# Sparse attention and Fourier mixing: batch 1's block sums and first mask on VectorE instead of GpSimd, its scaled sums on ScalarE instead of VectorE

## The chip, the cores and the metric

The kernel runs on one core of a Trainium2 chip. A core has a matmul engine (TensorE; PE in the profile, with its weight loads as PEld), VectorE (DVE), ScalarE (ACT), GpSimd (POOL) and SyncE (SP), which here issues nearly all DMAs. The metric is the device time of one execution in microseconds (us). The kernel before takes 800.13 us, the median of 3 runs (798.32 to 802.27).

## The reference

There are 4 batches of 8 heads, 768 tokens and 64 dimensions per head, in float32. The attention is local with a window of 16, plus one summary per block of 32 tokens: the key of a block is the maximum of its 32 keys, and its value is the mean of its 32 values. Its output, 768 tokens by 512 features, goes through a Fourier mixing, a normalisation and a two-layer network.

```
k_sum = k.reshape(B, H, nb, block, D).max(axis=3)
v_sum = v.reshape(B, H, nb, block, D).mean(axis=3)
scores_l = scale * np.matmul(q, k.transpose(0, 1, 3, 2))        # kept where |i - j| < 16
scores_s = scale * np.einsum('bhsd,bhnd->bhsn', q, k_sum) + np.log(block)
a = softmax over both;  x = a @ [v, v_sum], heads joined to (B, S, 512)
mixed = np.real(fft over tokens and features of x);  u = x + mixed
un = (u - mean) / sqrt(var + 1e-6)
out = u + relu(un @ w_ch1) @ w_ch2
```

The change touches how `v_sum` and the first masked local scores of batch 1 are computed.

## The kernel before, in words

Heads are handled in pairs (g = 0 to 3). Batch 0's attention (`first_attention`, L838) runs alone at the start, in blocks of 64 tokens; the other batches use blocks of 32 (`scores`, `sum_scores`, `scale_sums`, `values`, `gen_attention`). Batch 0's attention ends with the folding of its output for the Fourier transform (`fold_sequence`, `fold_halves`, `fold_ends`). Then the Fourier stage of batch 0 (`gen_fourier`, transforms `y` and `mx`, statistics, `norm`, transposes `unt` into `u`) runs interleaved with the conversion of the weights from 64-bit words (`convert`, L1069 to L1076) and with the attention of batch 1. After that, each batch's two-layer network runs interleaved with the attention of the next one.

`block_sums(b, gg)` (L610) serves the value sums for four heads, that is, for the pairs 2gg and 2gg+1. For b of 1 and more it fetches the values as 96 rows (4 heads by 24 blocks) in four pieces of 512 numbers (8 tokens each), `raw[0]` to `raw[3]`, and adds them on GpSimd: 0 and 1, 2 and 3, both results, and then the remaining 512 numbers by halving (256, 128, 64), to `vb`, 64 numbers for each block. `scale_sums` selects a pair's rows by a matmul (`sel`), and writes them to `vs` twice, multiplied by two columns of 0 and 1 (`half_of`): for batch 1 by one broadcast product on VectorE, for later batches by two activations with a scale on ScalarE. `values` uses `vs`.

`scores` computes the exponentials of the local scores on ScalarE and multiplies them by a mask (`near`). This product is on VectorE, except for pair 0 of batch 1, where it is on GpSimd (`gtt`, L569), queued behind the block sums (`marks["vbs", 1]`).

What sets the order of the work: the program is written in one order, and a planner fills each engine's queue from it, oldest ready operation first; a block under `high_priority` (the Fourier stage, 600) counts as older. A younger operation can go ahead of an older one that the planner takes as not ready yet. `manual_schedule` around `first_attention` keeps the order of its own TensorE and VectorE operations among themselves, but doesn't keep others from going between them. `issue_after(m)` queues operations behind a mark m on the same engine. DMAs through `fetch` (L551) keep their written order on SP's queue while `in_order` is set, as it is up to the first network stage. In that order, block sums (1, 0) are loaded behind the values of pair (1, 0), the tables `near` and `mirror`, two pieces of weights, and keys and queries of pair (1, 1); sums (1, 1) are loaded after the Fourier stage of batch 0 is written.

Records of `tt` have line L567 and those of `gtt` L570, whatever calls them; `fetch` has L553. The tiles tell them apart: `vb` and `vbs` are the block sums, `p<-p,near` the mask, `vs<-vs,half` the scaled product, `big<-x,norm` the normalised tile, `words` and `w` the weights.

Of the kernel before, what the change touches and what calls it, by code (L numbers as in the profile page):

```python
# [12 lines left out]
AF = mybir.ActivationFunctionType  # L13
ALU = mybir.AluOpType
AX = mybir.AxisListType

P = 128
# [473 lines left out]
def _main_program(ctx, tc, q, k, v, moe_w_ch1, moe_w_ch2, out):  # L491
# [59 lines left out]
    def fetch(out, in_):  # L551

        ins = nc.sync.dma_start(out=out, in_=in_)  # L553
        if in_order[0]:
            tc.keep_in_program_order(ins)
        return ins.ins
# [12 lines left out]
    def gtt(out, in0, in1, op):  # L569
        return nc.gpsimd.tensor_tensor(out=out, in0=in0, in1=in1, op=op).ins  # L570
# [39 lines left out]
    def block_sums(b, gg):  # L610

        heads, rows = slice(4 * gg, 4 * gg + 4), 4 * nb
        f = BLOCK // 4
        n = f * D
        vb = spool.tile([rows, D], FP, tag="vbs", bufs=2, name=f"vbs_{b}_{gg}")
        for g in (2 * gg, 2 * gg + 1):
            sums[b, g] = vb, sel[:, g % 2]
        src = v[b, heads].rearrange("h (n f) d -> (h n) (f d)", f=BLOCK)
        if b == 0:

            raw = words[0:rows, 4 * n * gg:4 * n * (gg + 1)]
            fetch(out=raw, in_=src)
            to_add[gg] = raw, vb
            return
        if done_weights:
            raw = room(f"vb_{b}_{gg}")
            raw = [raw[0:rows, n * i:n * (i + 1)] for i in range(4)]
        else:

            raw = [bpool.tile([P, NC, P], FP, tag="s", bufs=5, name=f"vb_{b}_{gg}_{i}").rearrange("p n t -> p (n t)")  # L630
                   [0:rows] for i in range(4)]
        for i in range(4):
            fetch(out=raw[i], in_=src[:, n * i:n * (i + 1)])

        gtt(raw[0], raw[0], raw[1], ADD)
        gtt(raw[2], raw[2], raw[3], ADD)
        gtt(raw[0], raw[0], raw[2], ADD)
        while f > 2:
            f //= 2
            gtt(raw[0][:, 0:f * D], raw[0][:, 0:f * D], raw[0][:, f * D:2 * f * D], ADD)  # L640
        marks["vbs", b] = gtt(vb, raw[0][:, 0:D], raw[0][:, D:2 * D], ADD)

# [124 lines left out]
    def scores(b, g):  # L769
        kt, qt = kt_bufs[g % 2], nat[b, g]  # L770
        ps = [abank([P, NB2, BLOCK], f"sc_{b}_{g}_{h}") for h in range(2)]
        for i in range(NB2):
            for h in range(2):
                o = BLOCK * (NB2 * h + i)
                for e in range(2):
                    rows, r = slice(D * e, D * (e + 1)), 64 * (e ^ h)
                    nc.tensor.matmul(ps[h][r:r + 64, i, :], kt[rows, o:o + 64], qt[rows, o:o + BLOCK],  # L777
                                     start=True, stop=True)
        p = apool.tile([P, 2, NQ, QB], FP, tag="p", name=f"p_{b}_{g}")
        pm = p[:, 1].rearrange("p n c -> p (n c)")[:, 0:S2]  # L780
        p = p[:, 0].rearrange("p (h i) (j c) -> p h (i j) c", h=2, c=BLOCK)
        for h in range(2):
            nc.scalar.activation(out=p[:, h], in_=ps[h], func=AF.Exp, scale=SC)
            with tc.issue_after(marks["vbs", 1]) if (b, g) == (1, 0) else ExitStack():
                (gtt if (b, g) == (1, 0) else tt)(p[:, h], p[:, h], near[:, h], ALU.mult)
        return p, pm

    def sum_scores(b, g, p):
# [8 lines left out]
    def scale_sums(b, g):  # L797
        ps = abank([P, D], f"vs_{b}_{g}")
        vb, pick = sums[b, g]
        nc.tensor.matmul(ps, pick, vb, start=True, stop=True)  # L800
        if b > 1:
            for r in range(2):
                nc.scalar.activation(out=vs[:, r, 0:D], in_=ps, func=AF.Identity, scale=half_of[:, r:r + 1])
        else:
            tt(vs[:, :, 0:D], ps[:, None, :].to_broadcast([P, 2, D]),
               half_of[:, :, None].to_broadcast([P, 2, D]), ALU.mult)

    def values(b, g, p, pm, x):
        vw = vw_bufs[g % 2]
# [28 lines left out]
    def first_attention():  # L838

        x = x_of[0] = bpool.tile([P, NST, DM], FP, tag="x", bufs=2, name="x_0")  # L840
        fold = bpool.tile([P, 7, 2, S2], FP, tag="u", name="fold_0").rearrange("p a k n -> p (a k n)")
        wt["fold"] = split_fold(0, fold)
        p = {0: wide_scores(0, 0, lambda: add_blocks(0))}
        prepare(0, 1)
        sum_values(0, 0)
        load(0, 3)
        for g in range(NP - 1):
            p[g + 1] = wide_scores(0, g + 1, (lambda: add_blocks(1)) if g == 1 else None)
            wide_values(0, g, p[g], x)
            load_values(*following(0, g, 2))  # L850
            for par in range(2):
                fold_sequence(par, g)
            if g < NP - 2:
                prepare(0, g + 2)
                sum_values(0, g + 1)
            if g == NP - 3:
                load(1, 0)
                get_tables(0, lambda: load_raw(1))
                load_raw(2)
                sum_values(0, g + 2)  # L860
        fold_halves(0, 0)
        wide_values(0, NP - 1, p[NP - 1], x)
        for par in range(2):
            fold_sequence(par, NP - 1)
            if par:
                fold_halves(par, 0)
            fold_halves(par, 1)
            for _ in fold_ends(0, par, wt["fold"][:, par], wt["fold"][:, 2 - 2 * par]):
                pass
# [96 lines left out]
    def gen_attention(b):  # L966
        x = bpool.tile([P, NST, DM], FP, tag="x", bufs=2, name=f"x_{b}")
        x_of[b] = x
        held = None
        if b == 2:  # L970
            load(2, 1)
            load(2, 2)
        if b > 1:
            yield
            yield
            with tc.issue_after(marks["load"]):
                block_sums(b, 0)
            for _ in range(2):
                yield
        for g in range(NP + 1):  # L980
            n1, n3 = (following(b, g, n) for n in (1, 3))
            if held:
                if b > 1:
                    scale_sums(b, g - 1)
                values(b, g - 1, *held, x)
                if n1 and b > 1:
                    load_values(*n1)
            if g == NP and b > 1:
                turn_tiles(b, x)
                for _ in range(17):  # L990
                    yield
                rooms[b] = room(f"fold_{b}")
                steps = fold_batch(b, split_fold(b, rooms[b]))
                while True:
                    with tc.issue_after(marks["dense"]):
                        done = next(steps, steps) is steps
                    if done:
                        break
                    yield
            elif held:  # L1000
                for _ in range(5 if b > 1 else 1):
                    yield
            if g < NP:
                held = scores(b, g)
                if (b, g) == (1, 1):
                    key_maxima(g)
                sum_scores(b, g, held[1])
            if g and n1 and b == 1:
                load_values(*n1)
            if g == 1 and b > 1:  # L1010
                block_sums(b, 1)
            if g == NP and b > 1:
                return
            yield
            if g == NP:
                return
            for _ in range(2 if g == 0 and b > 1 else 0):
                yield
            if n1:
                prepare(*n1, *((1,) if b > 1 else ()))  # L1020
            if b == 1:
                scale_sums(b, g)
            if b > 1:
                yield
                yield
                if n1:
                    prepare(*n1, 0)
            if n3 and not (b == 1 and n3 > (2, 0)):
                load(*n3)
            yield  # L1030
            if b > 1:
                yield
# [153 lines left out]
    def gen_fourier(b):  # L1186
# [45 lines left out]
        for half in range(2):  # L1232
# [46 lines left out]
            ins = nc.vector.tensor_tensor(out=z, in0=minus, in1=y, op=ALU.mult)  # L1279
            if b == 0:  # L1280
                marks["mx", 0] = ins.ins
            norms.append((y, z))
        issued.add(("mx", b))
        for j in range(3):
# [200 lines left out]
    weights = gen_weights()  # L1485
    with tc.manual_schedule(engines={mybir.EngineType.PE, mybir.EngineType.DVE}):
        first_attention()
    fetch(out=near, in_=dr["near"].ap().rearrange("p (h i) c -> p h i c", h=2))
    fetch(out=mirror, in_=dr["mirror"].ap())
    load_raw(4)  # L1490
    load(1, 1)
    nc.vector.memset(vs, 0.0)
    nc.vector.tensor_scalar(out=vs[:, :, D], in0=half_of, scalar1=float(BLOCK), scalar2=None, op0=ALU.mult)

    block_sums(1, 0)

    def second_attention():
        prepare(1, 0)
# [76 lines left out]
```

## Time and profile before

| | us |
|---|---|
| median of 3 runs | 800.13 (798.32 to 802.27) |
| the profiled execution | 801.87 |
| its span in the profile | 800.0 |
| TensorE busy in the span | 775.7 |
| VectorE busy | 499.2 |
| ScalarE busy | 229.0 |
| GpSimd busy | 60.9 |

The page gives busy time for each engine; TensorE's matmuls are pipelined, so its busy time isn't time at its peak. The rows of a timeline are: start (us from the span's start), duration, engine, line, operation, output tile <- input tiles with their shapes, and how often; in brackets stands how long the engine was idle before, and what ended that. A list of waits gives the engine, the tile and the line that waited, what it waited for, and us in total, times, and the longest. "Granted clock" is the share of TensorE's full clock. Windows of the span show the stages:

| stretch, us | TensorE busy | VectorE busy | ScalarE busy | GpSimd busy | granted clock |
|---|---|---|---|---|---|
| 48 to 60 (first transform) | 12.00 | 9.53 | 5.72 | 0 | 0.77 |
| 69 to 75 (statistics) | 5.96 | 5.97 | 1.77 | 4.13 | 1.00 |
| 75 to 80 (norm) | 0.21 | 5.00 | 0.86 | 3.08 | 0.74 |
| 80 to 94 (transposes, attention of pair 0) | 12.12 | 11.32 | 11.45 | 0 | 0.73 |
| 94 to 116 (network, first half) | 19.97 | 21.14 | 13.06 | 0 | 1.00 |
| 116 to 123 | 7.00 | 6.42 | 3.33 | 6.25 | 1.00 |
| 147 to 190 (first output stage) | 42.86 | 36.77 | 15.18 | 0 | 1.00 |

GpSimd's work from 69 to 78 us is block sums (1, 0) and the first mask of batch 1; from 116 to 123 us it is block sums (1, 1).

### The profile page before, as it was taken

To read this page: it belongs to the slowest core of one execution; us is meant where nothing else is said; L and a number is where in the kernel's file an instruction comes from. 1 tells how busy PE (TensorE), PEld (TensorE's weight loads), DVE (VectorE), ACT (ScalarE), POOL (GpSimd) and SP (SyncE) were. 2 spreads that over 40 slices of the span, in tenths; PEclk is the share of its full clock that TensorE was granted. 3 is DMA by queue.
4 is the path that set the end of the run, shared out by engine and by line. 5 is a ranking of instruction groups with operands and counts; after the bars stand their busy time and mean duration, and the time that the engine had idled before them with its cause. 6 is when DMAs were issued, how large, how long until landed. Compare 5 with 4: busy or idle time off the path is not lost.

```text
span 800.0 us, 14475 instructions
## 1 busy us (share of the span) xinstructions
PE 775.7 (97%) x5914; PEld 566.6 (71%) x5914; DVE 499.2 (62%) x1113; ACT 229.0 (29%) x515; POOL 60.9 (8%) x99
## 2 busy tenths in 40 slices
PE   8987899999999999999999999999999999999997
PEld 6776655445579866788569866688669875786686
DVE  5789898797988737663577635563576722532352
ACT  3542756445635112200226112210126102001200
POOL 0003011000000021200120020300030000000000
PEclk9989899999999999999999999999999999999999
DMA  9799596697756269985343169620613154106001
GB/s 227 170 270 206 158 275 174 233 252 263 214 164 173 68 171 208 251 137 138 134 174 138 54 198 194 176 82 1 229 57 139 46 189 144 70 0 231 0 28 55
DMA packets 133355, 121.84 MB, mean 152 GB/s; under 512 B 94464, under 2 KB 114912, under 8 KB 133088
## 3 DMA queue, kind: packets, MB, share of 16 engines
q1 hardware_dynamic: 132016, 118.53, 53.1%
q0 software_dynamic: 576, 2.10, 0.7%
q8 instruction: 48, 0.79, 0.4%
q10 hardware_dynamic: 688, 0.20, 0.1%
q14 instruction: 27, 0.22, 0.1%
HBM read 97.22 MB, written 23.59 MB: 151 GB/s over the span
## 4 chain that ended last, share of the span: by engine, by line
PE 85%; DVE 10%; ACT 3%; issue 1%; DMA 1%; ACTq 0%; DVEq 0%
PE hx L1325 19%; PE ox L1394 18%; PE hz L1325 9%; PE oz L1394 9%; PE oy L1394 5%; PE o L1371 4%; PE hy L1325 4%; PE y L1220 4%; PE mx L1179 2%; PE sc L777 2%; DVE w L567 2%; PE av L816 1%; PE unt L1299 1%; PE av L821 1%; DVE x L567 1%; DVE p L567 1%
## 5 line engine op out<-in xcount | busy, mean ns | idle before, releaser
L1325 PE MATMUL hx<-u,w 128*128 128x384 f32 x512 | 184.8, 490 | 4.9 <-DVE h L567 3.2
L1325 PEld LDWEIGHTS hx<-u,w 128*128 128x128 f32 x512 | 95.2, 190 | 73.7 <-DVE h L567 5.2
L1325 PE MATMUL hz<-u,w 128*128 128x384 f32 x256 | 93.5, 486 | 0.0
L1394 PE MATMUL oz<-w,s 128*128 128x256 f32 x336 | 81.5, 380 | 0.0
L1394 PE MATMUL ox<-w,s 128*128 128x256 f32 x336 | 80.3, 380 | 0.0
L1394 PE MATMUL ox<-w,h 128*128 128x256 f32 x336 | 79.9, 381 | 0.0
L567 DVE TENSOR_TENSOR x<-ox,x 128x256 f32<-128x256 f32 x84 | 35.4, 423 | 67.5 <-PE ox L1394 67.3
L1325 PEld LDWEIGHTS hz<-u,w 128*128 128x128 f32 x256 | 48.5, 190 | 34.3 <-ACT h L1344 0.9
L1394 PEld LDWEIGHTS ox<-w,h 128*128 128x128 f32 x336 | 63.0, 190 | 11.1 <-issue 1.2
L1394 PEld LDWEIGHTS ox<-w,s 128*128 128x128 f32 x336 | 63.0, 190 | 9.5 <-DVE x L567 0.8
L1394 PEld LDWEIGHTS oz<-w,s 128*128 128x128 f32 x336 | 63.4, 190 | 8.6
L1336 ACT COPY h<-hx 128x384 f32<-128x384 f32 x32 | 15.2, 476 | 184.6 <-PE hx L1325 184.6
L567 DVE TENSOR_TENSOR h<-hy,h 128x384 f32<-128x384 f32 x32 | 17.8, 556 | 47.3 <-PE hy L1325 47.2
L1325 PE MATMUL hy<-u,w 128*128 128x384 f32 x128 | 46.5, 486 | 0.0
L567 DVE TENSOR_TENSOR h<-hx,h 128x384 f32<-128x384 f32 x32 | 17.8, 556 | 43.3 <-PE hx L1325 43.2
L1371 PE MATMUL o<-w,h 128*128 128x512 f32 x96 | 42.2, 595 | 0.1
L1355 ACT ACTIVATE h<-hx 128x384 f32<-128x384 f32 x32 | 15.7, 491 | 88.4 <-PE hx L1325 88.4
L1394 PE MATMUL oy<-w,h 128*128 128x256 f32 x168 | 40.1, 380 | 0.0
L570 POOL TENSOR_TENSOR vb<-vb 96x512 f32<-96x512 f32 (+2 forms) x24 | 23.9, 997 | 179.7 <-DMA vb<-in_v_dram 178.3
L1325 PEld LDWEIGHTS hy<-u,w 128*128 128x128 f32 x128 | 24.3, 190 | 17.0
L567 DVE TENSOR_TENSOR x<-oz,x 128x256 f32<-128x256 f32 x42 | 17.8, 423 | 29.0 <-PE oz L1394 28.7
L1394 PEld LDWEIGHTS oy<-w,h 128*128 128x128 f32 x168 | 31.8, 190 | 4.4
(165 smaller groups left out, 1101.0 us busy)
## 6 DMA issues: line engine op xcount, KB each, us to landing
w<-dw SPq DMA_DIRECT2D x44, 896.0 KB, 5.6
words<-in_moe_w_ch_dram SPq DMA_DIRECT2D x32, 512.0 KB, 5.1
dw<-w SPq DMA_DIRECT2D x12, 896.0 KB, 6.9
vw<-in_v_dram SPq DMA_DIRECT2D x47, 192.0 KB, 5.7
out_dram<-x SPq DMA_DIRECT2D x23, 256.0 KB, 2.0
vb<-in_v_dram SPq DMA_DIRECT2D x24, 192.0 KB, 7.8
kn<-in_k_dram SPq DMA_DIRECT2D x9, 384.0 KB, 5.4
qn<-in_q_dram SPq DMA_DIRECT2D x9, 384.0 KB, 6.7
```

The source lines that it names most:

```text
L567: return nc.vector.tensor_tensor(out=out, in0=in0, in1=in1, op=op).ins
L570: return nc.gpsimd.tensor_tensor(out=out, in0=in0, in1=in1, op=op).ins
L777: nc.tensor.matmul(ps[h][r:r + 64, i, :], kt[rows, o:o + 64], qt[rows, o:o + BLOCK], start=True, stop=True)
L816: nc.tensor.matmul(av[r][32 * j:32 * (j + 1), t, :], p[rows, h, i - NB2 * h, :], vw[rows, i, :], start=(t == 0), stop=False, skip_group_ch ...
L821: ins = nc.tensor.matmul(av[r][:, t:t + HT + 1:HT, :], pm[rows, P * t:P * (t + 1)], vs[rows], start=False, stop=(t == HT - 1), skip_group_ ...
L1179: nc.tensor.matmul(out, y[:, g], table, start=False, stop=True, skip_group_check=True)
L1220: nc.tensor.matmul(y, fgs[b][par][:, st, P * g:P * (g + 1)], fs[par][:, g % 2, st, :], start=(st == 0), stop=(st == n - 1))
L1325: ins = nc.tensor.matmul(ps, w[:, a, kk, :], u[:, r, kk, :], start=start and kk == 0, stop=stop and kk == 1, skip_group_check=True)
L1336: nc.scalar.copy(out=c11, in_=X)
L1355: nc.scalar.activation(out=c21, in_=X, func=AF.Relu)
L1371: nc.tensor.matmul(ps, h[:, n, hf, P * t:P * (t + 1)], wt[2, b, j][:, 2 * hf:2 * hf + 2, :], start=(n, hf) == (0, 0), stop=(n, hf) == (NC ...
L1394: nc.tensor.matmul(ps, left[a][:, n, :], wt[2, b, j][:, r, :], start=start and n == 0, stop=stop and n == NC - 1, skip_group_check=True)
```

## The change

For batch 1 the block sums are added on VectorE: three additions of 96x512, and one reduction over the remaining 8 rows of 64 in place of the halving. For (1, 0) the loading and the adding are parted: the four loads are written in `first_attention` ahead of the loads of pair (1, 0)'s values, and the additions behind the end of `first_attention`, with no mark. For (1, 1) both stay where they were. The first mask of batch 1 moves to VectorE, behind the end of the norm of the first half (a new mark, `norm`), and is written after pair 0's scores and before the preparation of pair 1. The scaled sums of batch 1 are two activations on ScalarE, as in later batches. Later batches keep GpSimd for the block sums.

```diff
--- before.py
+++ after.py
@@ -631,14 +631,24 @@
                    [0:rows] for i in range(4)]
         for i in range(4):
             fetch(out=raw[i], in_=src[:, n * i:n * (i + 1)])
-
-        gtt(raw[0], raw[0], raw[1], ADD)
-        gtt(raw[2], raw[2], raw[3], ADD)
-        gtt(raw[0], raw[0], raw[2], ADD)
+        to_add[b, gg] = raw, vb
+        if (b, gg) != (1, 0):
+            add_later_blocks(b, gg)
+
+    def add_later_blocks(b, gg):
+        f = BLOCK // 4
+        raw, vb = to_add[b, gg]
+        add = gtt if b > 1 else tt
+        add(raw[0], raw[0], raw[1], ADD)
+        add(raw[2], raw[2], raw[3], ADD)
+        add(raw[0], raw[0], raw[2], ADD)
+        if b == 1:
+            nc.vector.tensor_reduce(out=vb, in_=raw[0].rearrange("p (f d) -> p d f", d=D), op=ADD, axis=AX.X)
+            return
         while f > 2:
             f //= 2
             gtt(raw[0][:, 0:f * D], raw[0][:, 0:f * D], raw[0][:, f * D:2 * f * D], ADD)
-        marks["vbs", b] = gtt(vb, raw[0][:, 0:D], raw[0][:, D:2 * D], ADD)
+        gtt(vb, raw[0][:, 0:D], raw[0][:, D:2 * D], ADD)
 
 
 
@@ -781,8 +791,8 @@
         p = p[:, 0].rearrange("p (h i) (j c) -> p h (i j) c", h=2, c=BLOCK)
         for h in range(2):
             nc.scalar.activation(out=p[:, h], in_=ps[h], func=AF.Exp, scale=SC)
-            with tc.issue_after(marks["vbs", 1]) if (b, g) == (1, 0) else ExitStack():
-                (gtt if (b, g) == (1, 0) else tt)(p[:, h], p[:, h], near[:, h], ALU.mult)
+            if (b, g) != (1, 0):
+                tt(p[:, h], p[:, h], near[:, h], ALU.mult)
         return p, pm
 
     def sum_scores(b, g, p):
@@ -798,12 +808,8 @@
         ps = abank([P, D], f"vs_{b}_{g}")
         vb, pick = sums[b, g]
         nc.tensor.matmul(ps, pick, vb, start=True, stop=True)
-        if b > 1:
-            for r in range(2):
-                nc.scalar.activation(out=vs[:, r, 0:D], in_=ps, func=AF.Identity, scale=half_of[:, r:r + 1])
-        else:
-            tt(vs[:, :, 0:D], ps[:, None, :].to_broadcast([P, 2, D]),
-               half_of[:, :, None].to_broadcast([P, 2, D]), ALU.mult)
+        for r in range(2):
+            nc.scalar.activation(out=vs[:, r, 0:D], in_=ps, func=AF.Identity, scale=half_of[:, r:r + 1])
 
     def values(b, g, p, pm, x):
         vw = vw_bufs[g % 2]
@@ -847,6 +853,8 @@
         for g in range(NP - 1):
             p[g + 1] = wide_scores(0, g + 1, (lambda: add_blocks(1)) if g == 1 else None)
             wide_values(0, g, p[g], x)
+            if g == NP - 2:
+                block_sums(1, 0)
             load_values(*following(0, g, 2))
             for par in range(2):
                 fold_sequence(par, g)
@@ -1016,6 +1024,10 @@
                 return
             for _ in range(2 if g == 0 and b > 1 else 0):
                 yield
+            if (b, g) == (1, 0):
+                for h in range(2):
+                    with tc.issue_after(marks["norm"]):
+                        tt(held[0][:, h], held[0][:, h], near[:, h], ALU.mult)
             if n1:
                 prepare(*n1, *((1,) if b > 1 else ()))
             if b == 1:
@@ -1279,6 +1291,7 @@
             ins = nc.vector.tensor_tensor(out=z, in0=minus, in1=y, op=ALU.mult)
             if b == 0:
                 marks["mx", 0] = ins.ins
+                marks["norm"] = marks.get("norm", ins.ins)
             norms.append((y, z))
         issued.add(("mx", b))
         for j in range(3):
@@ -1485,14 +1498,13 @@
     weights = gen_weights()
     with tc.manual_schedule(engines={mybir.EngineType.PE, mybir.EngineType.DVE}):
         first_attention()
+    add_later_blocks(1, 0)
     fetch(out=near, in_=dr["near"].ap().rearrange("p (h i) c -> p h i c", h=2))
     fetch(out=mirror, in_=dr["mirror"].ap())
     load_raw(4)
     load(1, 1)
     nc.vector.memset(vs, 0.0)
     nc.vector.tensor_scalar(out=vs[:, :, D], in0=half_of, scalar1=float(BLOCK), scalar2=None, op0=ALU.mult)
-
-    block_sums(1, 0)
 
     def second_attention():
         prepare(1, 0)
```

## The prediction

> **What bounds the kernel now.** I read the page first, for which engine is full, then the waits of TensorE, for where it is not.
>
> ```profile
> span 800.0 us, 14475 instructions
> PE 775.7 (97%) x5914; PEld 566.6 (71%) x5914; DVE 499.2 (62%) x1113; ACT 229.0 (29%) x515; POOL 60.9 (8%) x99
> ```
>
> TensorE stands still for 24.3 us of the span, so a change off TensorE can win only there, or where its clock is low. The waits of TensorE between 36 and 240 us have one long entry:
>
> ```profile
> PE unt L1299 <- DVE big L1294: 4.8, 1, 4.8
> PE hx L1325 <- DVE h L567: 2.5, 2, 1.4
> ...
> PE hx L1325 <- ACT h L1336: 1.7, 2, 1.1
> ```
>
> The first is batch 0's normalisation: TensorE ends its earlier work at 74.96 us (keys and queries of pair 1, which begin at 74.14 for 0.82) and turns the first normalised tile at 79.79. Third view, the timeline of VectorE and of GpSimd there (start, duration, engine, line):
>
> ```profile
> 69.58 0.91 DVE L1267 TENSOR_SCALAR stat<-both 128x3 f32<-128x3 f32 x1
> 70.40 0.15 DVE L1268 TENSOR_SCALAR stat<-both 128x3 f32<-128x3 f32 x1
> ...
> 72.14 1.14 DVE L567 TENSOR_TENSOR norm<-norm,stat 128x3 f32<-128x3 f32 x1
> ...
> 73.80 0.83 DVE L1278 SCALAR_TENSOR_TENSOR norm<-norm 128x3 f32<-128x3 f32 x1
> ...
> 76.18 2.08 DVE L1278 SCALAR_TENSOR_TENSOR norm<-norm 128x3 f32<-128x3 f32 x1
> ```
> ```profile
> 69.19 1.27 POOL L570 TENSOR_TENSOR vb<-vb,vb 96x512 f32<-96x512 f32 x1 [26.71 <-DMA vb<-in_v_dram]
> 71.98 2.63 POOL L570 TENSOR_TENSOR vb<-vb,vb 96x512 f32<-96x512 f32 x2 [1.52 <-DMA vb<-in_v_dram]
> ...
> 76.30 1.94 POOL L570 TENSOR_TENSOR p<-p,near 128x384 f32<-128x384 f32 x2
> ```
>
> Operations on three elements take 0.14 to 0.17 us when GpSimd is idle (L1268: 0.15), but four of them last until the GpSimd instruction beside them ends: 70.49 against 70.46, 78.26 against 78.24. The norm, and with it TensorE, stands behind the very work that this change takes off GpSimd. The chain that ended last runs through all four.
>
> **The stalls go.** (0.91-0.15) + (1.14-0.14) + (0.83-0.15) + (2.08-0.15) = 4.37 us. What is late next: the last of the matmuls that these sums read ends at 71.21 us (it starts at 70.18 and takes 1.03), and VectorE, relieved of the first two stalls, reaches the operation that reads it at 73.20-1.76 = 71.44, so it still doesn't wait; and TensorE is busy to 74.96 while the first tile would be ready at 79.79-4.37 = 75.42. So the whole 4.37 counts: -4.4.
>
> **Block sums of pairs 0 and 1 on VectorE.** Three additions of 96x512 and one reduction of 512 elements. The rows, first by group and shape (times, total us, mean ns of one, idle before), then by tile for the mask and for the product on ScalarE (minimum, median, maximum ns):
>
> ```profile
> L686 DVE TENSOR_REDUCE km<-kt 128x24 f32<-128x768 f32 x16 | 15.1, 944 | 0.3 <-ACT kt L713 0.3
> ...
> L567 DVE TENSOR_TENSOR words<-words 96x512 f32<-96x512 f32 x2 | 1.4, 686 | 0.1
> ```
> ```profile
> L567 DVE TENSOR_TENSOR p<-p,near x22: 548/551/1618, 96.7 to 526.4; 128x384 f32<-128x384 f32 x22
> ```
> ```profile
> L803 ACT ACTIVATE vs<-vs,half x16: 308/316/320, 302.8 to 528.1; 128x64 f32<-128x64 f32 x16
> ```
>
> A reduction of 512 with stride is not in the trace: from below 0.944 x 512/768 = 0.63, from above 0.944; I take 0.69, as an addition of 512 costs. So 4 x 0.69 = 2.7 us. They take the place of halving additions whose rows are 0.42, 0.29 and 0.22 (0.93 together).
> The Trainium skill, "VectorE: DVE Perf Modes", section "Rules for kernel authors", calls tensor_reduce the slowest VectorE operation and advises restructuring. By it the halving would stay, at 3 x 0.69 + 0.93 = 3.0 us instead of 2.7. The rows speak for the change: over 768 elements a reduction takes 0.944 us and an addition (L567, u) 0.950.
> Where do the first 2.7 us lie? Between the end of batch 0's folding (53.35) and the first sum of the norm (65.20) VectorE idles 2.20+0.38+0.71+0.55 = 3.84 us, by the waits in its timeline (ACT's conversions, then TensorE). That hides 2.7 us of work, but not a wait for the data as well. Data: the loads move ahead of the values' loads. The weights' load before them, issued at 39.90, lands 13.0 us later, at 52.9; 0.79 MB more at the 214 to 335 GB/s seen from 54 to 60 us lands at 55.3 to 56.6, if served in order. Additions that stand right behind the folding then wait 2 to 3.2 us: 2.7+3.2-3.84 = 2.1 at most, 0 at least; I take +0.5. Behind them the values' loads (used at 82.86), the mask (used at 76), the keys of pair 1 (used at 73.43) start some 3 us later: they landed by 59, 58.2 and 67.5, so this is hidden; without that cover each would cost its own lateness.
>
> **Sums (1,1), at 116 us.** GpSimd's work there stretches six VectorE operations by 0.24+1.08+1.07+0.53+0.25+0.12 = 3.3 us (against their rows of 0.42, 0.69, 0.68); 2.7 come instead: -0.6 on VectorE. TensorE waits 1.08 us for VectorE at 128.93. Between 0 and -1.1: I take -0.3.
>
> **Masks.** Two of 0.55 us, queued behind the first half's norm. Between 0 (in VectorE's 0.51 us wait at 80.93, and before the matmuls that need them at 82.86) and 1.1 (ahead of the first tile): +0.2.
>
> **Product on ScalarE.** Two of 0.316 for one of 0.285 on VectorE, four times. In the stretch 79.1 to 89.0 ScalarE never rests except 0.34+0.21 us waiting for TensorE's transposes, and the norm's further tiles and bank releases queue behind it: 0.63-0.55 = +0.1. The next, beside the copies of keys and queries at 92.8 to 97.0 after which TensorE waits 0.58 for ScalarE, 0 to 0.6; the last two 0 to 1.3, hidden under dense TensorE from 147 to 190 for one; together +0.3.
>
> **Clock.** The granted clock falls to 0.50 from about 77.5 us, 2.5 us into the wait, and is back at 1 by 88. Twelve transposes take 2.84 us at 79.79 and 1.66 at 87.37. With the wait near 0.4 us the clock should hold; ScalarE bounds that stretch, so of 1.2 I take -0.3 (from 0 to -3.5, half of the 7.08 us that TensorE worked from 80 to 88).
>
> Batches 2 and 3 keep their instructions; I cost them at nothing, since TensorE covers them (99% from 229 us on).
>
> **Sum.** -4.4 +0.5 -0.3 +0.2 +0.1 +0.3 -0.3 = -3.9 us. The profiled execution took 801.87 us (span 800.0, 1.87 around it): 798.0. It lies 1.74 above the median of the runs shown, 800.13, so against that: 796.2.
>
> **Rivals.** *Slower: the additions stand too early in VectorE's queue.* They bear no ordering tie to the folding, only the rule that the planner may fill an engine when an older operation is not ready. The trace shows both halves: VectorE's norm chain has later tiles' statistics threaded into it (L1254 between L1268 and L1271), and at the start VectorE waits 6.7 us, to 8.89, for a tiny load (L1493) with the first key maxima behind it. If the additions are planned for 44 to 50 us, VectorE stands until 55.3 to 56.6, and batch 0's folding, the first transform (TensorE from 48.09) and all else behind it: 5 to 12 us plus 2.7 of work, less the wait of 4.4 won: +3 to +10, about 805. It decides as soon as one addition stands ahead of the folding's last operation (52.88). Against it: the folding leaves VectorE 0.16 us of idle from 42 to 48 and none from 48 to 53, so hardly a place to fill.
> *Given back at 107 to 116.* The same for sums (1,1): their loads are issued from 107.26 and GpSimd starts only at 116.16 on the data. Additions planned at 111 to 113 hold VectorE 3 to 5 us, of which TensorE, with little slack there (2.5 us of waits for VectorE), sees about 3: 799.2.
> *More is won:* the clock holds, ScalarE's and TensorE's small waits from 80 to 98 (1.9 + 0.6 us) close too: -7, 793.
> *It doesn't do what it says:* the stretching came from something else than GpSimd. The ends that agree to 0.03 us speak against it; I give it nothing of its own and count it with the second (800).
>
> **Numbers.** Forecast 0.45 (794.5 to 798); more won 0.13 (791 to 794.5); given back 0.20 (798 to 801); slower 0.22 (801 to 810). A measurement here tells about 0.5%, 4.0 us, from no change: faster is below 796.1, slower above 804.1. A little over half of the forecast's chance (0.25) and all of "more won" are faster: 0.38; most of the slower case is slower: 0.20; the rest is within: 0.42. Leaving out a little over half of the slower case and the end of the best gives 792.3 to 805; the likeliest case's own range, 794.5 to 798, stands beside it.
>
> **What would show it.** Right: TensorE's wait before the first transpose under 1 us, the three-element operations all near 0.15, the clock at 1 from 78 to 88, VectorE waiting under 3.2 us for the sums' data. Wrong: a VectorE wait for that data before 53 us or near 110, or masks ahead of the first tile. The forecast falls if the planner's order of batch 0's end changes.

## The result, and the profile after

The changed kernel takes 805.14 us (median of 15 runs, 801.79 to 810.11), the kernel before beside it 800.13 (15 runs, 797.33 to 804.22). The ratio is 1.0057, with a 95% interval of 1.0036 to 1.0077: slower, where the forecast was 3.9 us faster. The profiled execution took 806.53 us, its span is 804.7.

The page of the changed kernel, its span and its engines:

```profile
span 804.7 us, 14470 instructions
PE 779.7 (97%) x5914; PEld 568.9 (71%) x5914; DVE 496.4 (62%) x1119; ACT 231.5 (29%) x523; POOL 47.3 (6%) x85
```

The work has moved as meant: GpSimd is busy for 13.6 us less. But TensorE, with the same 5914 matmuls, is busy for 4 us more, so a part of them ran at a lower clock (the mean granted clock is 0.986, before 0.988).

The waits of TensorE between 36 and 240 us (total, times, longest):

```profile
PE unt L1312 <- DVE norm L1288: 3.2, 1, 3.2
PE vs L810 <- ACT kt L723: 2.2, 3, 1.5
...
PE sc L787 <- ACT qt L723: 1.4, 1, 1.4
```

The wait before the first transposes did not shrink to 0.4 us, it went from 4.8 to 3.2; and a new one is there, for ScalarE's copies of the keys (kt). VectorE at the norm, in time:

```profile
78.50 0.15 DVE L567 TENSOR_TENSOR norm<-norm,stat 128x3 f32<-128x3 f32 x1
...
78.71 0.15 DVE L1290 SCALAR_TENSOR_TENSOR norm<-norm 128x3 f32<-128x3 f32 x1
...
78.97 0.56 DVE L567 TENSOR_TENSOR p<-p,near 128x384 f32<-128x384 f32 x1
...
79.52 0.54 DVE L1307 TENSOR_SCALAR big<-x,norm 128x512 f32<-128x512 f32 x1
```

All three-element operations take 0.13 to 0.17 us: the stalls are gone. From the first sum x<-mx (69.37) to the first tile of big it is 10.15 us, before 13.99 (65.20 to 79.19). One mask stands ahead of that tile. So the norm did win about 4 us against that one execution of the kernel before. What became of them is in TensorE's and ScalarE's timelines:

```profile
76.16 0.85 PE L804 MATMUL ss<-qt,km 64*32 64x384 f32 x8
80.21 2.79 PE L1312 MATMUL unt<-ident,big 128*128 128x128 f32 x12 [3.20 <-DVE norm L1288]
82.79 0.99 PE L721 MATMUL qk<-ident,kn 128*128 128x128 f32 x6
...
85.98 0.43 PE L810 MATMUL vs<-vbs,sel 96*128 96x64 f32 x2 [1.54 <-ACT kt L723]
87.05 2.55 PE L822 MATMUL av<-vw,p 64*32 64x65 f32 x96 [0.63 <-issue]
...
91.23 2.56 PE L1312 MATMUL unt<-ident,big 128*128 128x128 f32 x12
```
```profile
79.09 0.81 ACT L1304 ACTIVATE big<-x,norm 128x512 f32<-128x512 f32 x1 [1.53 <-DVE norm L1291]
82.24 0.59 ACT L1313 COPY u<-unt 128x512 f32<-128x512 f32 x1 [2.33 <-PE unt L1312]
...
85.44 1.51 ACT L723 COPY kt<-qk 64x384 f32<-64x384 f32 x3
86.97 2.07 ACT L723 COPY qt<-qk 64x384 f32<-64x384 f32 x4
```

The order has changed. Before, TensorE turned the keys and queries of pair 1 (qk) ahead of the first transposes, from 73.43 to 74.96 us, and ScalarE had copied one piece at 74.02. Now qk comes behind them, at 82.79; ScalarE is idle for 1.53 and 2.33 us first, and copies kt and qt only until 89.0. The loads of that pair were issued at 60.91 and 61.66 and landed 8.0 and 8.6 us later, so the data had lain there 7 us when TensorE fell idle at 77.01. The first values (av) and the second transposes behind them run at half clock.

There is a second difference, at the start, with the same order of instructions:

```profile
10.78 0.17 DVE L1507 TENSOR_SCALAR vs<-half 128x2 f32<-128x2 f32 x1 [8.61 <-DMA half<-c_half]
10.86 0.95 DVE L696 TENSOR_REDUCE km<-kt 128x24 f32<-128x768 f32 x1
```

The load of `half` came 1.9 us later than before, the first key maxima stood behind it, TensorE waited 2.9 us for them, its clock fell to 0.5, and the third group of batch 0's values stood at 45.71 us instead of 41.05. So in these two profiles 4.66 us were lost before 46 us, 1.4 were won back by the last sum of the program (798.41 against 795.13, 3.28 later), and 1.4 more were lost between that sum and the end of the span. Two executions can't say which of these is the program's own. That is what the experiments are for.

### The profile page after: what moved, and what is told of

It is laid out like the page before. It is cut to its first block, busy times and chain, and to the rows that moved or that the text cites. A ratio compares the mean times of both kernels' runs of the same rounds, so it can differ in the third digit from the quotient of the medians.

```text
span 804.7 us, 14470 instructions
## 1 busy us (share of the span) xinstructions
PE 779.7 (97%) x5914; PEld 568.9 (71%) x5914; DVE 496.4 (62%) x1119; ACT 231.5 (29%) x523; POOL 47.3 (6%) x85
## 4 chain that ended last, share of the span: by engine, by line
PE 86%; DVE 9%; ACT 2%; DMA 1%; issue 1%; ACTq 0%; DVEq 0%
PE hx L1338 19%; PE ox L1407 18%; PE hz L1338 9%; PE oz L1407 9%; PE hy L1338 5%; PE o L1384 5%; PE oy L1407 5%; PE y L1232 3%; PE mx L1191 2%; PE sc L787 2%; PE av L822 2%; PE unt L1312 2%; DVE w L567 1%; PE av L827 1%; DMA half<-c_half 1%; DVE x L567 1%
## 5 line engine op out<-in xcount | busy, mean ns | idle before, releaser
L1384 PEld LDWEIGHTS o<-w,h 128*128 128x128 f32 x96 | 17.9, 190 | 22.9 <-issue 20.5
```

Of the source, the lines that this page charges most:

```text
L1384: nc.tensor.matmul(ps, h[:, n, hf, P * t:P * (t + 1)], wt[2, b, j][:, 2 * hf:2 * hf + 2, :], start=(n, hf) == (0, 0), stop=(n, hf) == (NC ...
```

## The experiments

Eighteen runs in five groups. Each group ran on one chip beside the kernel before; between groups I compare the ratios to it. All these kernels compute the whole reference.

**First group: is it the start or the order?** r1 is the changed kernel again. e1 pins TensorE's old order:

```
+                    if (b, g) == (1, 1):
+                        marks["prep"] = ins.ins      # last transpose of prepare(1, 1)
...
-            with tc.issue_after(marks["av", 1, 0]) if b == 0 and half else ExitStack():
+            with tc.issue_after(marks["av", 1, 0] if half else marks["prep"]) if b == 0 else ExitStack():
```

e2 takes the write that waits for `half` off the start, and e3 does both:

```
+    with tc.issue_after(marks["fold", 0]):
         nc.vector.tensor_scalar(out=vs[:, :, D], in0=half_of, ...)
```

Expected of r1:

> The changed kernel once more, unaltered, for its start. Two theories of the 4.66 us by which it stood behind before its first values were done (45.71 against 41.05 us, with the same order of instructions): by the first, the small load of `half`, which landed at 10.68 instead of 8.79 us, came late by chance in that one execution; then it lands nearer 8.8 here, TensorE's wait for the key maxima is nearer 0.5 than 2.9 us, and the first attention's third group of values stands nearer 41 us. By the second it belongs to this program: it lands at 10.5 us or later again, and the values stand near 45.7 us. The time by both: 805 us.

Expected of e1:

> The changed kernel with TensorE's old order: the turning of batch 1's second pair (qk(1,1)) ahead of the first transposes. My theory, that the planner's new order gives the norm's gain back: TensorE does qk(1,1) from about 77.0 to 78.5 us (counted with the late start), its wait before the first transposes falls from 3.2 to about 1.6 us, ScalarE copies kt and qt of that pair in its idle 1.5 and 2.3 us, and the second transposes end about 4 us sooner: 3 to 4.5 us less than the changed kernel, 800.5 to 802 us. The rival, that the order costs nothing because the wait for the norm is the same and only the place of 1.6 us of work differs: at most 1 us less, 804 to 805 us.

Expected of e2:

> The changed kernel with the write of the ones column (vs from half) put behind the first batch's folding, so that the first key maxima don't stand behind the load of `half`. If the late start belongs to this program, this takes 4 to 5 us off: 800 to 801 us, with no wait of TensorE for the key maxima over 0.3 us and a granted clock of 1 from about 14 us on. If it was chance, the median falls by no more than about 1 us: 804 to 805 us.

Expected of e3:

> Both edits together. If both theories hold, the two gains add: 8 us less than the changed kernel, 796 to 798 us, ahead of the kernel before by 2 to 4 us. If only the order matters, as in the run with the order alone, 800.5 to 802; if only the start matters, 800 to 801; if neither, 804 to 805.

Measured (kernel before 801.38): r1 804.79 (ratio 1.0062, 1.0038 to 1.0087); e1 800.73 (1.0012, 0.9991 to 1.0032); e2 801.04 (1.0003, 0.9985 to 1.0021); e3 800.02 (0.9984, 0.9968 to 1.0001).

In r1's profile `half` was written at 9.28 us, TensorE waited 0.3, and the third values stood at 41.44: the late start of the first profile was chance in that execution. The median is 805 again; but the profiled execution itself, with the load in time, took 802.01 us, the lowest of the six. e1 gives 4.1 us back, as the order theory said. e2 gives 3.8 back too, and both together only 4.8 (by the ratios 4.0, 4.7 and 6.2): the two gains don't add, so something was not understood, and I went on to single parts.

**Second group: what was there to win?** r2 is the kernel before again; e4 is it with e2's edit at the start; e5 is e3 with the product back on VectorE; e6 is e4 with the change's masks alone.

Expected of r2:

> The kernel before once more, unaltered, for its norm and its tail. If the four GpSimd stalls of the norm (0.76, 1.00, 0.68 and 1.93 us) belong to this program, the first tile of big follows the first sum x<-mx by 14 us again (65.20 to 79.19), against 10.2 in the changed kernel's repeat. If they were much of a chance, it follows by 11 to 13 us. From the last sum's start to the span's end: 4.9 us as before if that belongs to the program, about 6.2 us, as in all changed kernels so far, if it was chance.

Expected of e4:

> The kernel before with the same edit at the start as the run without the start's wait: the ones column is written behind the folding. It gives the change's worth free of the load of `half`. If that load was late in about half of the runs of either kernel, this falls 1 to 3 us below the kernel before, to 798 to 800 us, with a spread of some 3 us in place of 8; and with the order restored (800.0 us with this same edit) the change is then worth nothing or less than nothing. If the late load is the changed kernel's own, this is no faster than the kernel before, 800 to 801.5 us.

Expected of e5:

> The run with the old order and the start's edit, with the product of batch 1 back on VectorE. In that run ScalarE worked from 75.1 to 82.8 us almost without a stop, and the first values' last part waited 0.5 us for its two scalings (vs). My theory, that with the norm's stalls gone ScalarE is the next bound and the two scalings lie on its path: 0.5 to 1 us less, 799.0 to 799.6 us, with that wait gone. The rival, that the scalings are hidden: 800.0 us within 0.3.

Expected of e6:

> The kernel before with the start's edit and only the mask of the change: its two products on VectorE behind the norm, GpSimd keeps the sums, TensorE keeps its order. The stall of 1.93 us that the masks made goes, the sums' three (2.44 us together) stay, one mask (0.56) stands ahead of the first tile: the first tile of big follows the first sum by 12.4 to 12.9 us. If the norm's end still sets the time behind it, it is 1.0 to 1.4 us less than the kernel before with the start's edit alone; if ScalarE or the planner takes it back, within 0.5 us of that.

Measured (kernel before 800.19): r2 798.9 in its one run; e4 799.36 (0.9997, 0.9976 to 1.0018); e5 798.99 (0.9984, 0.9962 to 1.0006); e6 797.33 (0.9973, 0.9952 to 0.9995).

r2 is the run that corrects the forecast's base. GpSimd and then VectorE at the norm, in the kernel before:

```profile
65.16 1.27 POOL L570 TENSOR_TENSOR vb<-vb,vb 96x512 f32<-96x512 f32 x1 [22.28 <-DMA vb<-in_v_dram]
66.66 2.62 POOL L570 TENSOR_TENSOR vb<-vb,vb 96x512 f32<-96x512 f32 x2 [0.23 <-DMA vb<-in_v_dram]
...
73.05 1.96 POOL L570 TENSOR_TENSOR p<-p,near 128x384 f32<-128x384 f32 x2 [1.99 <-ACT p L783]
```
```profile
73.40 0.68 DVE L567 TENSOR_TENSOR norm<-norm,stat 128x3 f32<-128x3 f32 x1
...
74.15 0.88 DVE L1278 SCALAR_TENSOR_TENSOR norm<-norm 128x3 f32<-128x3 f32 x1
...
75.96 0.55 DVE L1294 TENSOR_SCALAR big<-x,norm 128x512 f32<-128x512 f32 x1
```

In the execution that the forecast was read from, the first addition began at 69.19 us and the second waited 1.52 us for its data; here the data of the first were there 4 us earlier, and all additions are done at 71.06. What is left are stalls of 0.27 (an operation of 0.41 at 70.26), 0.53 and 0.73: 1.5 us, not 4.4. From first sum to first tile it is 11.0 us, and so in the later profiles that keep masks and sums on GpSimd (p4, f3 and g2 11.0, f4 10.7, e4 12.9): 13.99 was the largest of seven, of which two are of the kernel before itself. TensorE waits 1.9 us in r2, and its clock stays at 1 from 66 to 94 us, where in the first profile it had fallen to 0.5.

e6 wins 2.0 us on e4 (12 runs each on one chip; the intervals of the two ratios overlap). The times of e5 and e3 can't be compared, since the chips differ; their ratios are the same, within intervals of some 2 us, so this pair tells nothing of the product.

**Third group: the parts, one by one, on the kernel before.** p1 has only the masks; p2 masks and product; p3 only the sums (early loads, additions on VectorE, the second sums too); p4 only the place of the four loads, with all additions on GpSimd:

```
             wide_values(0, g, p[g], x)
+            if g == NP - 2:
+                block_sums(1, 0)                     # p4: the four loads only
...
     with tc.manual_schedule(engines={mybir.EngineType.PE, mybir.EngineType.DVE}):
         first_attention()
+    add_later_blocks(1, 0)                           # p4: still gtt, as before
...
-    block_sums(1, 0)
```

Expected of p1:

> The kernel before with one part of the change: only the two masks of batch 1's first pair on VectorE behind the norm. My theory now, that the mask alone pays and the other parts cost: 2 to 3 us less than the kernel before (which has had medians of 800.1 to 801.4), with the granted clock of most runs at 0.995 or more. The rival, that the gain of 2 us seen with the start's edit came from a reorder by the planner: within 1 us of the kernel before.

Expected of p2:

> The kernel before with two parts: the mask on VectorE and the product on ScalarE, the block sums as they were. Theory: the product costs 1 us, as with the old order (799.0 with it on VectorE, 800.0 on ScalarE), so 1 us above the run with the mask alone and still 1 to 2 us under the kernel before. Rival: the product is hidden, the same as the mask alone within 0.4 us.

Expected of p3:

> The kernel before with the third part alone: the four loads of batch 1's first block sums ahead of its first values, the adds on VectorE ahead of the norm, the second sums on VectorE too; the mask stays on GpSimd, the product on VectorE. TensorE's order is the changed kernel's (first transposes ahead of qk(1,1)). Theory, that this part carries the loss: 2.5 to 5 us more than the kernel before. Rival, that the loss needs the parts together: within 1 us of the kernel before.

Expected of p4:

> The kernel before with the place of the four loads alone changed: ahead of batch 1's first values; all adds and the mask stay on GpSimd. TensorE's order is again the changed kernel's. If the order that comes with the place of the loads makes the loss, 2.5 to 4 us more than the kernel before, as the sums alone; if VectorE's 5 us of adds make it, no loss here: GpSimd is done with the adds before the norm, only the mask's stall is left, and the time is that of the kernel before or 1 us less.

Measured (kernel before 800.09): p1 799.23 (0.9997, 0.9975 to 1.0018); p2 801.03 (1.0013, 0.9994 to 1.0033); p3 804.77 (1.0063, 1.0034 to 1.0091); p4 805.72 (1.0062, 1.0036 to 1.0088).

This is the turning point: four loads at another place in SP's queue, with their additions still on GpSimd and only written earlier, cost as much as the whole change. In p4 GpSimd is done with the additions well before the norm, and VectorE has none of them. The masks alone are worth less here than in e6 (no difference that this can tell); the product adds 1.8 us to p1, with intervals that overlap.

**Fourth group: the order, made and unmade without the rest.** f3 is the kernel before with the loads of pair 1 four places later in SP's queue, behind the four loads of the block sums; these come two places earlier by it (issued from 53.99 us, in r2 from 56.97), and nothing else moves. f1 is the whole change with those two loads taken ahead; f2 is f1 with the product back on VectorE; f4 is p4 with e2's edit at the start.

```
f3, on the kernel before:                f1, on the changed kernel:
     load_raw(4)                              add_later_blocks(1, 0)
-    load(1, 1)                          +    load(1, 1)
...                                           fetch(out=near, ...)
     block_sums(1, 0)                    ...
+    load(1, 1)                               load_raw(4)
                                         -    load(1, 1)
```

Expected of f1:

> The whole change, with the two loads of batch 1's second pair (kn and qn) taken ahead of the mask table and the words in SP's queue. The planner then turns the pair on TensorE and begins its copies on ScalarE ahead of the first transposes, as in the kernel before. If the order made the loss: 3 to 5 us less than the changed kernel, 800 to 802 us, with the second transposes ending some 3 to 5 us sooner after the first values than in the changed kernel. If the early loads themselves, or the start, make it: 804 to 805.5 us.

Expected of f2:

> The same with the product back on VectorE, so of the change the sums and the mask only. If the order made the loss and the product costs about 1 us: 799 to 801 us, about 1 us under the run with the product on ScalarE. If not the order: 803 to 804.5 us.

Expected of f3:

> The kernel before with one move: the loads of batch 1's second pair behind the four loads of the block sums, four places later in SP's queue. Nothing is loaded earlier, all adds and the mask stay on GpSimd. The planner makes the changed kernel's order out of it. If the order makes the loss: 3 to 5 us more than the kernel before, 803 to 805.5 us. If the early loads make it by what they do in the queues or at the start: 800 to 801.5 us, as the kernel before.

Expected of f4:

> The kernel with the four loads early and nothing else changed (805.7 us), with the ones column behind the folding, so without the start's wait. If the order makes the loss, it stays above the kernel before with the same edit (799.4) by 2.5 to 4 us: 802 to 803.5. If the late load of `half` makes it, it comes down to 799 to 800.5 us. Of the 3.8 us that this edit took off the changed kernel, the share that was the start's shows here a second time.

Measured (kernel before 800.98): f1 797.23 (0.9958, 0.9936 to 0.9981); f2 794.82 (0.9931, 0.9909 to 0.9952); f3 803.94 (1.0056, 1.0032 to 1.0080); f4 803.92 (1.0046, 1.0027 to 1.0066).

f3 makes the loss by this exchange of places alone, with its norm as long as in r2 (11.0 us). f1, with every other part of the change in place, goes from 1.0057 to 0.9958, some 8 us. f4 keeps the loss with the start's wait gone. Order, then, in the main, and not the additions. Of the start f4 takes 1.3 us off p4 by the ratios, which their intervals don't tell from nothing.

**Fifth group: controls.** g2 is the kernel before with f1's move alone; g1 is f2 with e2's edit at the start.

Expected of g2:

> The kernel before with the loads of batch 1's second pair ahead of the mask table and the words, nothing else. TensorE's and ScalarE's orders stay those of the kernel before. If the gain of 6 us in the run with the sums, the mask and this move is the change's own (no GpSimd beside the norm), this is the kernel before within 1 us: 799.5 to 801.5. If the earlier pair makes it, 795 to 797.

Expected of g1:

> The sums and the mask of the change, the pair's loads first, the product on VectorE, and the ones column behind the folding. The late load of `half` was in three of the six profiles of kernels with early loads that keep the column where it was. If it costs 1 to 2 us in the mean and the planner moves nothing else: 793 to 794.5 us against 794.8 without this edit, with less spread; if the planner's other moves outweigh it, 795 to 797.

Measured (kernel before 801.73): g2 799.63 (0.9988, 0.9970 to 1.0006); g1 794.23 (0.9914, 0.9894 to 0.9933; 6 runs). Moving the pair's loads ahead wins nothing measurable by itself, so what f2 has below g2 (0.9931 against 0.9988, some 4.6 us) comes with the sums and masks on VectorE and their early loads. It isn't the norm's stalls, though: from TensorE's first matmul of mx to the first tile f2's profile takes 15.35 us, g2's 15.54. The difference lies behind: from the first to the second transposes f2 takes 4.42 us and g2 6.85. ScalarE and TensorE of f2:

```profile
74.76 1.52 ACT L723 COPY kt<-qk 64x384 f32<-64x384 f32 x3
76.34 0.81 ACT L1308 ACTIVATE big<-x,norm 128x512 f32<-128x512 f32 x1
```
```profile
77.36 1.53 PE L1316 MATMUL unt<-ident,big 128*128 128x128 f32 x12 [1.11 <-DVE big L1311]
...
81.78 1.53 PE L1316 MATMUL unt<-ident,big 128*128 128x128 f32 x12 [0.84 <-ACT big L1308]
```

Here ScalarE's order differs once more: three copies of the keys come ahead of the norm's tile, in g2 (shown next) only one, and g2's TensorE then waits 1.71 us for the copies of the queries. So a part of the 4.6 us may again be order; no run separates it.

g1 is the fastest version of this study, ahead of both kernels; its lead over f2 is within the intervals. (Its expectation counts the late loads of `half` wrongly: it was four of seven profiles.)

g2 and f3 differ in the place of two loads alone. TensorE and ScalarE of g2, where the pair's loads are issued at 50.03 and 51.38 us:

```profile
73.24 0.88 PE L711 MATMUL qk<-ident,kn 128*128 128x128 f32 x6
73.95 0.82 PE L711 MATMUL qk<-ident,qn 128*128 128x128 f32 x6
76.64 1.53 PE L1299 MATMUL unt<-ident,big 128*128 128x128 f32 x12 [1.87 <-DVE big L1294]
...
83.49 1.78 PE L1299 MATMUL unt<-ident,big 128*128 128x128 f32 x12
```
```profile
73.82 0.52 ACT L713 COPY kt<-qk 64x384 f32<-64x384 f32 x1
75.96 0.81 ACT L1291 ACTIVATE big<-x,norm 128x512 f32<-128x512 f32 x1 [1.62 <-DVE norm L1279]
76.80 1.56 ACT L713 COPY kt<-qk 64x384 f32<-64x384 f32 x3
...
81.82 1.00 ACT L713 COPY qt<-qk 64x384 f32<-64x384 f32 x2
```

And of f3, where they are issued at 57.01 and 57.55 and land 9.8 and 12.1 us later, near 67 and 70 us:

```profile
76.67 2.79 PE L1299 MATMUL unt<-ident,big 128*128 128x128 f32 x12 [3.40 <-DVE norm L1278]
79.25 1.19 PE L711 MATMUL qk<-ident,kn 128*128 128x128 f32 x6
...
82.67 0.41 PE L800 MATMUL vs<-vbs,sel 96*128 96x64 f32 x2 [1.58 <-issue]
...
86.82 1.53 PE L1299 MATMUL unt<-ident,big 128*128 128x128 f32 x12
```
```profile
75.90 0.81 ACT L1291 ACTIVATE big<-x,norm 128x512 f32<-128x512 f32 x1 [2.08 <-DVE norm L1279]
78.70 0.58 ACT L1300 COPY u<-unt 128x512 f32<-128x512 f32 x1 [1.99 <-PE unt L1299]
...
83.62 2.06 ACT L713 COPY qt<-qk 64x384 f32<-64x384 f32 x4
```

The first tile is begun at the same time (76.0 us). In g2 TensorE fills the wait with qk and ScalarE has copied one of the eight pieces before the norm ends and four by 78.4; in f3 TensorE stands still for 3.4 us, its clock falls, the transposes take 2.79 instead of 1.53 us, ScalarE idles 2.08 and 1.99 us, and its last copy ends at 85.7 instead of 82.8. The second transposes begin 3.3 us later, and the last sum of the program 4.2 (796.02 against 791.85). The granted clock in two of the stretches of f3 (the third number from the end):

```profile
76.00:78.00 2.00, 1.33 (x7) 1.36 (x8) 1.61 (x7) 0.71 (x1) 0.00 (x0) 0.65 0.00 1
78.00:80.00 2.00, 2.00 (x11) 2.00 (x10) 1.43 (x6) 1.09 (x2) 0.00 (x0) 0.50 0.03 8
```

In g2 it is 1.00 in both.

## Why the prediction was wrong, point by point

**The step that failed first: the loads that fall behind others in SP's queue were taken as "hidden", at no cost.** The prediction wrote that the keys of pair 1 would start some 3 us later and that this was hidden since they had landed long before their use. The data were indeed in time. But the place of a load in SP's queue also decides where the planner puts the work that uses it, on TensorE and on ScalarE: f3 and p4 each make the new order and the loss by the place of loads alone, f1 undoes both. The price is 0.0056 by f3 against the kernel before, 4.5 us. The forecast named the condition ("falls if the planner's order of batch 0's end changes") and gave it neither a chance nor a price. How the planner reckons is not in a trace; that it reckons with the place in the queue is what f1, f3 and p4 show.

**The stalls, -4.4: right in kind, and one execution's size.** They went, all four, and the norm of that profile was shortened by 13.99 - 10.15 = 3.84 us. But the repeat shows 1.5 us of stalls, and 11.0 us as the usual length: about 0.9 us to win on the path, because one mask (0.56) now stands ahead of the first tile. The block sums take 0.66 of that back ahead of the norm (below). Counted from TensorE's first matmul of mx the first tile stands after 15.34 us in r1 and 15.55 in r2, so 0.2 us is won; in the first pair of profiles it was 3.2 (15.33 against 18.51). The prediction saw that the profiled execution lay 1.74 us above the median, and took the 3.9 off the median all the same. A stall whose length depends on when a load lands has to be priced with that load's spread. The Trainium skill, "SBUF — State Buffer", section "Who interferes with whom", says that a VectorE operation with two SBUF inputs and a GpSimd operation that reads SBUF exclude each other for a whole instruction; the rows agree (0.88 and 0.68 us beside the masks, 0.15 without). One of the four stalled operations of the first profile (L1267, 0.91 us) reads one tile only, and that sentence says nothing of it.

**"The whole 4.37 counts".** It took TensorE as busy to 74.96 with qk ahead of the transposes. That order was the cover of the wait, and it was lost.

**Block sums, +0.5: about right.** The additions waited for no data; they sit between the conversions from 62.8 to 68.3 us. But VectorE has no idle time left for them all. The first matmul of mx and the first sum, before and after:

```profile
60.68 1.46 PE L1247 MATMUL mx<-fd,big 128*128 128x256 f32 x6
65.20 1.89 DVE L567 TENSOR_TENSOR x<-mx,x 128x512 f32<-128x512 f32 x3 [0.55 <-PE mx L1249]
```
```profile
64.19 1.46 PE L1259 MATMUL mx<-fd,big 128*128 128x256 f32 x6
69.37 1.88 DVE L567 TENSOR_TENSOR x<-mx,x 128x512 f32<-128x512 f32 x3
```

Before, the sum begins 4.52 us after the matmul, and VectorE has waited 0.55 for TensorE; after, 5.18 us, with VectorE busy up to it: 0.66 us later. The eight profiles whose block sums are loaded behind the values show 4.51 or 4.52, the ten with the additions on VectorE 5.17 to 5.19. The reduction was outside its bounds (0.63 to 0.944):

```profile
L646 DVE TENSOR_REDUCE vbs<-vb x2: 1021/1026/1032, 67.3 to 128.3; 96x64 f32<-96x512 f32 x2
```

It reads with a stride, where the row it was bounded by reads in a line. The halving that it replaces would have taken 0.93 by the prediction's rows; the rule of the Trainium skill that it weighed and set aside ("VectorE: DVE Perf Modes", "Rules for kernel authors") was the better guide, by 0.1 us.

**Sums at 116 us, -0.3; the rival of their waiting for data.** They ran at 125 to 129 us with no such wait. Neither gain nor loss shows.

**Product on ScalarE, +0.1 and +0.3: too low.** With the order restored, ScalarE is the next bound, and the scalings lie on its path. The waits of TensorE in f1, from 70 to 96 us:

```profile
PE av L827 <- ACT vs L812: 1.4, 1, 1.4
PE unt L1312 <- DVE big L1307: 1.1, 1, 1.1
```

The first has no counterpart in f2. The difference of the two kernels is 2.4 us, of p2 and p1 1.8; each pair's intervals overlap. I put it at 1 to 2.5 us, a fourth to a half of what the order costs.

**Masks, +0.2.** One of the two did stand ahead of the first tile (0.56 us), as the prediction named for a sign of being wrong. The masks on VectorE win 2.0 us in e6 against e4, but nothing that can be told in p1, so what they are worth by themselves isn't settled.

**Clock, -0.3.** It should have held at 1 from 78 to 88 us. It fell in the wait of 3.2 us and again behind the copies.

**Rivals.** The slower rival (additions ahead of the folding) did not happen; the loss came by a way that no rival held. That 805.14 is near its "about 805" is chance. "Given back" expected the loss of the gain from additions on VectorE near 110 us; it came from TensorE's and ScalarE's order near 77.

**The account.** With the pair's loads ahead in both kernels, the one with sums and masks on VectorE is 4.6 us faster (f2 against g2). That is about the size forecast, but by luck: the norm, from which the forecast took it, gives 0.2 us in their two profiles, and ScalarE's order an unknown part. The product costs 1 to 2.5, and the order some 4.5 us by f3. By f1 against the whole change it is 8, of which 1.5 lie behind the last sum: in the changed kernel (both profiles) and in e1 to e3 the span ends 6.0 to 6.4 us after that sum begins, in all the others, f1 among them, after 4.6 to 4.9. No engine's work is shown there; the cause stays open. f1 also has f2's better order on ScalarE. Put together, 4.5 + 1.5 + (1 to 2.5) - 4.6 gives 2.4 to 3.9 us of the 4.6 that the change lost; each part is known to some 2 us only.

**What stays open.** Why e2's edit took 3.8 us off the changed kernel, while it took 1.3 off p4 (f4, by the ratios) and 0.2 off the kernel before (e4, by the ratio; 0.8 by the medians). A part may be the start: the 21 runs of the changed kernel took either 801.8 to 803.7 us (ten) or 805.1 to 810.1 (eleven), and of the two profiled ones the one with the late load took 806.53, the other 802.01; two profiles don't show it. The order of some work further on differs in e2 as well: of the two profiles, r1's falls 1.2 us behind between 110 us and the last sum. And the start: `half` was written after 10.7 us in four of seven profiles of kernels with the early loads (10.74 to 11.35), in none of six without (8.70 to 9.28), though the orders agree up to there. r1 shows that it is not fixed for a program; whether it is likelier in some is not settled. f1's profile has it late and still took 797.86 us.

## What to carry to other kernels

A load that is moved ahead in a queue moves others back, and a planner that reckons with a load's place in the queue, as this one does, can then reorder engines that the edit never names: compare the order of every engine before pricing anything, and if it changed, move the neighbour's load as well rather than give up the edit. Price a stall from more than one execution when its length hangs on a load's landing. When a stall goes, look at which engine has the next full stretch before giving it more work.

## What the runs showed that I had not expected

- A strided reduction of 512 elements (96x64 out of 96x512) takes 1.02 us, longer than one of 768 elements in a line (0.944).
- How much GpSimd and the norm collide varies between executions of one kernel: from first sum to first tile the kernel before took 14.0 and 11.0 us in its two profiles, and kernels with masks and sums on GpSimd 10.7 to 12.9 in five more. TensorE's clock went down to 0.5 behind it in the first, and stayed at 1 from 66 to 94 us in r2.
- The length of a wait of TensorE doesn't settle the clock behind it. Waits of 3.2 and 3.4 us before the transposes were followed by 0.50 (r1, f3), but one of 3.75 left it at 1.00 up to 80 us, through those transposes (e4, 1.56 us). r2 and g2 wait nearly alike (1.87 us, then 1.68 and 1.71): r2 stays at 1, g2 is at 0.50 from 82 to 84 us. At 0.50 the twelve transposes take 2.79 us instead of 1.53.
- The data of a load of 1 KB at the start were used between 8.70 and 11.35 us, in kernels with the same instructions up to there.
